# Sixteen rows of the first key load issued by ScalarE, and two w_down pieces placed ahead of the carried sum

## The chip, the core and the metric

The kernel runs on one core of one Trainium2 chip. The metric is device time in microseconds (us), the median of several executions. Beside it stands one execution that was taken with the hardware profiler. Its trace is what every duration below comes from.

## What is computed

The program is one decode step of a parallel block: `out = x + attention(xn) + glu(xn)`, with `xn` the layer norm of `x`. There are 2 batch rows of 512 values, 32 heads of 128, and attention looks at the last 2,048 positions of a key and value cache. Everything is f32. Cut to what matters:

```python
xn = layernorm(x)                                  # (2, 1, 512)
q  = (xn @ wq) split into 32 heads of 128
k, v = k_cache[:, :, 8192 - 2048:, :], v_cache[:, :, 8192 - 2048:, :]
p  = softmax(einsum("bhqd,bhkd->bhqk", q, k) * 128 ** -0.5)
a  = einsum("bhqk,bhkd->bhqd", p, v)  ->  (2, 1, 4096) @ wo
b  = ((xn @ w_gate) * (xn @ w_up)) @ w_down        # 512 -> 1376 -> 512
return x + a + b
```

Nearly all of the data is the keys and values: 2 MB for the keys of one head (both batch rows) and 2 MB for its values, each byte used once.

## The kernel before, in words

All operands except `x` in its natural layout are packed on the host into one flat `stream`, in the order in which they are loaded. `loads()` lists the loads, `placed()` says where each lands in three large SBUF tiles (`step0` to `step2`, the list `ring`), and `issue(name)` (line 486) starts one load on Sync's queue. Every load is a block of 128 rows, one for each SBUF partition.

The 32 heads are worked in 8 groups of 4. One turn of the loop at line 673 handles the keys of group `it` and the values of the group before. For a key of one head VectorE multiplies the whole tile by the query (`products`, 128 x 4096 values in place) and sums over the head dimension (`sums`). TensorE projects the queries (`project`), weighs the values (`weigh`, accumulating in PSUM tile `o_ps`), picks out the diagonal (`gather`) and multiplies by `wo` (`wo`, accumulating in PSUM tile `acc`). ScalarE computes the exponentials and copies.

Loads go in a ring: a later load overwrites the place of keys or values already used, so its issue on Sync waits for the engine that read them last. Each group of heads takes three loads of 6,144 KB. The first loads differ:

- `x` (1,057 KB): the first group of `wq`, and the small constant block with `x` transposed. Everything in the prologue (lines 516 to 539: mean, variance, `xn`, `xnb`) and the first query projection waits for it.
- `0.0` (6,080 KB): the keys of heads 0 and 1 (K0 and K1), and part of `w_gate` (`GU_A`). One of its 128 rows is 47.5 KB.
- `0.1` (5,568 KB): the keys of head 2, and the rest of `w_gate` and `w_up`.

The program is first recorded as a list of operations with their dependences, and `emit` then writes it out. `plan` works out which semaphores each operation waits for. A load with a tag (`B0`, `B1`, `B2`) counts on a semaphore shared by one place of the ring; a load without one gets a semaphore of its own. In `emit`, line 332 writes Sync's first three operations, the loads `x`, `0.0` and `0.1`, ahead of Sync's branch into its long straight block (`with nc.body("straight", ...)`, line 341). All of ScalarE's operations stand in its straight block; the first of them is the load of `x` in natural layout into `xr` (line 496, two rows of 2 KB), which waits for GpSimd's clearing of `xr`.

At the end, after the last group, Sync issues four small loads: `wo` (the last group's) and `d0` (pieces 1 to 4 of `w_down`), 1,024 KB each, `d1` (pieces 7 and 8, 512 KB) and `d2` (piece 9, 256 KB). The section `tail` (line 748) then runs in this order:

```python
    for j, i in enumerate(ROWS):                 # pieces 1 to 4, from d0
        down(i, add_rows, j, last=True)          # into acc
    dve.tensor_tensor(acc_sb, acc, xr, op=ALU.add)
    add_groups(id4, acc_sb)                      # the carried sum, into acc_g
    for i in STRIPS:                             # pieces 7, 8 (d1) and 9 (d2)
        down(i, add_groups, last=(i == STRIPS[-1]))
    dve.tensor_copy(o_out, acc_g)
```

`acc` holds four partial sums in four strips of partitions. VectorE adds `x` and moves them to SBUF (`acc_sb`), and a matrix product with `id4` adds the four strips together in `acc_g`, which lies in the PSUM tile of the queries (`q` in the profile). Each call of `add_groups` is four matrix products, one for each quarter of the output columns; the profile lists two TensorE instructions for each f32 product. The output is copied and stored by Sync.

Of the kernel before, what the change touches and what calls it, by code (L numbers as in the profile page):

```python
# [10 lines left out]
P = 128  # L11
# [18 lines left out]
EARLY, ROWS, STRIPS = (0, 5, 6, NFC), (1, 2, 3, 4), (7, 8, 9)  # L30
# [124 lines left out]
class Program:  # L155
# [131 lines left out]
    def emit(self, looped, control):  # L287
        nc, ops = self.nc, self.ops
        waits, at = self.plan(looped)
        stores = [i for i, o in enumerate(ops) if o.dma and o.args[0].space == bass.MemoryType.DRAM]  # L290
        sem = {}
        for late in (False, True):
            for i, o in enumerate(ops):
                if i in at and (i in stores) == late and o.tag not in sem:
                    sem[o.tag] = nc.alloc_semaphore(f"s_{o.tag}")
        regs = {}

        def give(i, first=None):
            o = ops[i]
            e = self.eng[o.eng]  # L300
            w = [(sem[ops[j].tag], at[j]) for j in waits[i]]
            if o.holds:
                w += [(sem[tag], regs[reg]) for tag, _, reg in o.holds]
            for s, v in w[:-1]:
                e.wait_ge(s, v)
            ins = o.call(e)
            if w:
                ins._wait_ge(*w[-1])
            if i in at:
                ins.then_inc(sem[o.tag], 16 if o.dma else 1)  # L310

        sections = {}
        for i, o in enumerate(ops):
            if o.eng == "PE":
                sec = sections.setdefault(o.place[0], {})
                if o.place in sec:
                    assert o.same(ops[sec[o.place]]), o.place
                    assert [t[::2] for t in o.holds] == [t[::2] for t in ops[sec[o.place]].holds]
                    assert (i in at) == (sec[o.place] in at)
                else:  # L320
                    sec[o.place] = i

        def run(section, *cut):
            got = list(sections[section].values())
            for i in got[cut[0] if cut else 0 : cut[1] if len(cut) > 1 else len(got)]:
                give(i)

        own = {e: [i for i, o in enumerate(ops) if o.eng == e] for e in self.eng}
        kinds = {"DVE": mybir.EngineType.DVE, "SP": mybir.EngineType.SP,
                 "ACT": mybir.EngineType.Activation}  # L330
        once = {}
        for i in own["SP"][:3]:
            give(i)
        for e in kinds:
            once[e] = self.eng[e].alloc_register(f"once_{e}")
            self.eng[e].reg_mov(once[e], 1)
            self.eng[e].br("straight")
        for i in own["POOL"]:
            give(i)
        self.eng["POOL"].br("done")  # L340
        with nc.body("straight", valid_engines=list(kinds.values())):
            for e in kinds:
                here = self.eng[e].mark_branch_hint_location()
                for i in own[e][3 if e == "SP" else 0 :]:
                    if i not in stores:
                        give(i)
                if e == "ACT":
                    far = here
                    self.eng[e].br_lt(once[e], 1, on_true="never", on_false="end")
                else:  # L350
                    if e == "SP":
                        self.eng[e].addr_align(128, offset=16, max_nops=0)
                    self.eng[e].br_lt(
                        once[e], 1, on_true="straight", on_false="end"
                    ).branch_hint(here)
        with nc.body("end", valid_engines=list(kinds.values())):
            for e in kinds:
                self.eng[e].br("done")
        control(self, regs, run)
        with nc.body("never", valid_engines=[kinds["ACT"]]):  # L360
            self.eng["ACT"].addr_align(128, offset=16, max_nops=0)
            self.eng["ACT"].br_lt(
                once["ACT"], 1, on_true="straight", on_false="done"
            ).branch_hint(far)
        nc.switch_bb("done")
        for i in stores:
            give(i)
        sp = self.eng["SP"]
        nums = sorted(s.num for t, s in sem.items() if t not in {ops[i].tag for i in stores})
        sp.sem_clear(range(nums[0], nums[-1] + 1))  # L370
        for i in stores:
            sp.wait_ge(sem[ops[i].tag], 16)
        for i in stores:
            n = sem[ops[i].tag].num
            sp.sem_clear(range(n, n + 1))
# [62 lines left out]
def build(nc, stream, x_nat, out):  # L438
    pr = Program(nc)
    pe, dve, act, pool = pr.pe, pr.dve, pr.act, pr.pool  # L440

    ring = [pr.sb(f"step{i}", [P, w]) for i, w in enumerate(TILES)]
# [36 lines left out]
    src, pos, tag_of = {}, 0, {}  # L479
    for name, (tag, _) in loads().items():  # L480
        t, lo, hi = spans[name]
# [1 line left out]
        pos += P * (hi - lo)  # L483
        tag_of[name] = tag

    def issue(name):
        t, lo, hi = spans[name]
        pr.load("SP", ring[t][:, lo:hi], src[name], tag=tag_of[name])

    issue("x")  # L490
    issue("0.0")
    issue("0.1")
    for t, v in ((mean_w, 1.0 / D), (eps_t, EPS), (ones, 1.0), (p_all, 0.0),
                 (xr, 0.0), (zero, 0.0), (mt, 0.0)):
# [18 lines left out]
    for t in (acc, *gu_ps):  # L513
        act.activation(t, ones[:, 0:1].to_broadcast([P, FB]), AF.Copy, scale=0.0,
                       tag="fold" if t is acc else "fold2")
# [22 lines left out]
        tag="qc",  # L538
# [94 lines left out]
    def add_groups(lhsT, rhs, last=False):  # L633
        nonlocal n_grp
        for j in range(4):
            pe.matmul(
                acc_g[32 * j : 32 * j + B, :], lhsT, rhs[:, j * P : (j + 1) * P],
                start=(n_grp == 0), stop=last,
            )
        n_grp += 1  # L640

    def down(c, add, *args, **kw):
        k = min(P, F - c * P)
        add(hT[:k, c % 4, c // 4, :], got["wd", c][:k], *args, **kw)
# [104 lines left out]
    for j, i in enumerate(ROWS):  # L749
        down(i, add_rows, j, last=True)  # L750
    dve.tensor_tensor(acc_sb, acc, xr, op=ALU.add)
    add_groups(id4, acc_sb)
    for i in STRIPS:
        down(i, add_groups, last=(i == STRIPS[-1]))
    dve.tensor_copy(o_out, acc_g)
    pr.load("SP", out, o_out)
    pr.emit(("q", "t", "g", "o", "w"), steer)
# [82 lines left out]
```

## Time and profile before

| | us |
|---|---|
| median of 3 runs | 376.68 |
| lowest and highest | 376.46, 378.28 |
| the profiled execution's own time | 376.57 |
| its span (first to last instruction) | 375.2 |

| engine | busy us | share of the span |
|---|---|---|
| VectorE (DVE) | 299.4 | 80% |
| TensorE matmul (PE) | 175.9 | 47% |
| TensorE weight load (PEld) | 54.8 | 15% |
| ScalarE (ACT) | 18.3 | 5% |
| GpSimd (POOL) | 3.0 | 1% |

How to read the lines below. Nearly all instructions are recorded through one helper, so nearly all carry its line, L139; they are told apart by their tiles. In a timeline line the first number is the start in us, the second the time from the first to the last of the group. `step` is the ring of loaded data, `step<-in_stream_dram` a load from the stream, `SPq` and `ACTq` the issuing queues of Sync and ScalarE. `q1` is the DMA queue that Sync's loads run on and `q10` ScalarE's; both are served by the same 16 DMA engines. A line of a windows view gives the stretch, its length, the busy time and the count of instructions of each engine, the granted TensorE clock, the mean busy share of the 16 DMA engines, and GB/s; it puts a packet where it starts, so a short stretch can show a share above 1.

### The profile page before, as it was taken

To read this page: it belongs to the slowest core of one execution; us is meant where nothing else is said; L and a number is where in the kernel's file an instruction comes from. 1 tells how busy PE (TensorE), PEld (TensorE's weight loads), DVE (VectorE), ACT (ScalarE), POOL (GpSimd) and SP (SyncE) were. 2 spreads that over 40 slices of the span, in tenths; PEclk is the share of its full clock that TensorE was granted. 3 is DMA by queue.
4 is the path that set the end of the run, shared out by engine and by line. 5 is a ranking of instruction groups with operands and counts; after the bars stand their busy time and mean duration, and the time that the engine had idled before them with its cause. 6 is when DMAs were issued, how large, how long until landed. Compare 5 with 4: busy or idle time off the path is not lost.

```text
span 375.2 us, 2080 instructions
## 1 busy us (share of the span) xinstructions
PE 175.9 (47%) x850; PEld 54.8 (15%) x850; DVE 299.4 (80%) x151; ACT 18.3 (5%) x42; POOL 3.0 (1%) x16
## 2 busy tenths in 40 slices
PE   0664743337416184064923277061740545343876
PEld 0210121002101030010400032010300112011322
DVE  0089999998599796997699985997969975999911
ACT  4000200000000000000000000000000000000000
POOL 3000000000000000000000000000000000000000
PEclk9965859587855688565695858566965869556899
DMA  9999999999999999999999999999999999999996
GB/s 365 415 456 403 447 419 419 466 456 419 419 419 419 461 461 419 419 419 419 461 461 419 419 419 419 445 472 424 419 419 419 440 477 424 419 443 394 449 401 249
DMA packets 4756, 159.62 MB, mean 425 GB/s; under 512 B 530, under 2 KB 658, under 8 KB 916
## 3 DMA queue, kind: packets, MB, share of 16 engines
q1 hardware_dynamic: 4752, 159.62, 98.8%
q10 hardware_dynamic: 4, 0.00, 0.0%
HBM read 159.55 MB, written 0.07 MB: 425 GB/s over the span
## 4 chain that ended last, share of the span: by engine, by line
DMA 49%; DVE 47%; PE 3%; issue 0%; SPq 0%; DVEq 0%
DMA step<-in_stream_dram 49%; DVE step L139 23%; DVE s L139 22%; PE q L139 2%; DVE rs L139 1%; PE acc L139 1%; SPq L139 0%; DVE acc_sb L139 0%; DVE h_sb L139 0%; PE top L139 0%; DVE nm L139 0%; DVE o_out L139 0%; DVE mt L139 0%; DVE dg L139 0%; DVE mtt L139 0%
## 5 line engine op out<-in xcount | busy, mean ns | idle before, releaser
L139 DVE TENSOR_TENSOR step<-step,q 128x4096 f32<-128x4096 f32 x32 | 141.3, 4414 | 41.7 <-DMA step<-in_stream_dram 41.7
L139 PE MATMUL o_ps<-step,p 128*32 128x512 f32 x512 | 93.0, 878 | 156.8 <-DMA step<-in_stream_dram 154.4
L139 DVE TENSOR_REDUCE s<-step 128x32 f32<-128x4096 f32 x32 | 141.3, 4417 | 0.8
L139 PEld LDWEIGHTS o_ps<-step,p 128*32 128x32 f32 x512 | 18.6, 146 | 219.0 <-DMA step<-in_stream_dram 171.7
L139 PE MATMUL q<-step,xnb 128*128 128x512 f32 x72 | 41.6, 732 | 9.0 <-DVE step L139 6.3
L139 PEld LDWEIGHTS q<-step,xnb 128*128 128x128 f32 x72 | 16.4, 240 | 28.0 <-issue 18.0
L139 PE MATMUL gu<-step,xn 128*2 128x512 f32 (+1 forms) x48 | 14.6, 774 | 11.7 <-DMA step<-in_stream_dram 11.7
L139 ACT COPY o_sb<-o_ps 128x256 f32<-128x256 f32 x16 | 5.2, 375 | 247.3 <-PE o_ps L139 247.3
L139 PE MATMUL gu<-step,o_sb 128*128 128x8 f32 x64 | 10.1, 285 | 4.0 <-ACT o_sb L139 4.0
L139 PEld LDWEIGHTS gu<-step,o_sb 128*128 128x128 f32 x64 | 9.4, 225 | 16.2 <-ACT o_sb L139 16.2
L139 ACT ACTIVATE p<-s,zero 64x128 f32<-64x128 f32 x16 | 6.4, 399 | 63.6 <-DVE s L139 63.5
L139 PE MATMUL acc<-step,oT 128*2 128x512 f32 x64 | 8.3, 592 | 0.4 <-DVE oT L139 0.4
L139 DVE TENSOR_REDUCE nm<-top 64x4 f32<-64x8 f32 x16 | 2.6, 164 | 6.8 <-PE top L139 6.7
L139 DVE RECIPROCAL rec<-tot 128x8 f32<-128x8 f32 x8 | 1.6, 198 | 6.2 <-PE tot L139 6.2
L139 PEld LDWEIGHTS gu<-step,xn 128*2 128x2 f32 x48 | 2.8, 98 | 23.3 <-DMA step<-in_stream_dram 13.4
L139 PE MATMUL top<-dg,ones 128*128 128x16 f32 x16 | 3.0, 260 | 7.0 <-DVE dg L139 7.0
L139 DVE TENSOR_REDUCE st<-xc 128x4 f32<-128x16 f32 x1 | 0.2, 169 | 6.3 <-POOL xc L139 6.3
L139 DVE TENSOR_TENSOR oT<-gu,rec 128x8 f32<-128x8 f32 x8 | 1.2, 156 | 4.3 <-PE gu L139 4.3
L139 PEld LDWEIGHTS top<-dg,ones 128*128 128x128 f32 x16 | 2.5, 188 | 12.8 <-DVE dg L139 11.8
L139 DVE TENSOR_REDUCE rs<-p 128x8 f32<-128x256 f32 x8 | 3.3, 412 | 0.9 <-ACT p L139 0.9
L139 ACT ACT_TABLE_LOAD x3 | 3.8, 1283 | 3.1 <-POOL xr L139 3.1
L139 PE MATMUL top<-st,mean_w 128*128 128x4 f32 x2 | 0.6, 364 | 6.5 <-DVE st L139 6.5
(44 smaller groups left out, 31.8 us busy)
## 6 DMA issues: line engine op xcount, KB each, us to landing
step<-in_stream_dram SPq DMA_DIRECT2D x20, 6144.0 KB, 30.5
step<-in_stream_dram SPq DMA_DIRECT2D x2, 4096.0 KB, 23.8
step<-in_stream_dram SPq DMA_DIRECT2D x1, 6080.0 KB, 19.0
step<-in_stream_dram SPq DMA_DIRECT2D x1, 5568.0 KB, 31.7
step<-in_stream_dram SPq DMA_DIRECT2D x1, 5120.0 KB, 29.8
step<-in_stream_dram SPq DMA_DIRECT2D x2, 2048.0 KB, 21.8
step<-in_stream_dram SPq DMA_DIRECT2D x2, 1024.0 KB, 11.6
step<-in_stream_dram SPq DMA_DIRECT2D x1, 1057.0 KB, 4.9
```

Of the source, the lines that this page charges most:

```text
L139: return getattr(engine, self.method)(*self.args, **self.kw)
```

## The change

There are two edits. The first: ScalarE, as its first operation and ahead of its branch, issues rows 0 to 15 of load `0.0` (on a semaphore of its own), while Sync issues `x`; Sync then issues the remaining 112 rows of `0.0` (on the shared semaphore `B0`), and `0.1`. The second: in the tail, pieces 7 and 8 of `w_down` are multiplied before the carried sum rather than after it; piece 9 stays last.

```diff
@@ -329,8 +329,10 @@
         once = {}
-        for i in own["SP"][:3]:
-            give(i)
+        first = {"ACT": 1, "SP": 3}
+        for e, n in first.items():
+            for i in own[e][:n]:
+                give(i)
         for e in kinds:
             once[e] = self.eng[e].alloc_register(f"once_{e}")
@@ -341,7 +343,7 @@
                 here = self.eng[e].mark_branch_hint_location()
-                for i in own[e][3 if e == "SP" else 0 :]:
+                for i in own[e][first.get(e, 0) :]:
                     if i not in stores:
                         give(i)
@@ -483,12 +485,14 @@
-    def issue(name):
+    def issue(name, eng="SP", rows=slice(0, P)):
         t, lo, hi = spans[name]
-        pr.load("SP", ring[t][:, lo:hi], src[name], tag=tag_of[name])
-
+        tag = tag_of[name] if rows.stop == P else None
+        pr.load(eng, ring[t][rows, lo:hi], src[name][rows], tag=tag)
+
+    issue("0.0", "ACT", slice(0, 16))
     issue("x")
-    issue("0.0")
+    issue("0.0", rows=slice(16, P))
     issue("0.1")
@@ -749,9 +753,10 @@
     dve.tensor_tensor(acc_sb, acc, xr, op=ALU.add)
+    for i in STRIPS[:-1]:
+        down(i, add_groups)
     add_groups(id4, acc_sb)
-    for i in STRIPS:
-        down(i, add_groups, last=(i == STRIPS[-1]))
+    down(STRIPS[-1], add_groups, last=True)
     dve.tensor_copy(o_out, acc_g)
```

## The prediction

> **What bounds the kernel now.** I read the page's DMA part first, then the windows, the waits behind the costliest groups, and the timeline at both ends of the span.
>
> ```profile
> span 375.2 us, 2080 instructions
> ...
> q1 hardware_dynamic: 4752, 159.62, 98.8%
> ...
> L139 DVE TENSOR_TENSOR step<-step,q 128x4096 f32<-128x4096 f32 x32 | 141.3, 4414 | 41.7 <-DMA step<-in_stream_dram 41.7
> ```
>
> Sync's queue keeps the 16 DMA engines busy for 98.8% of the span, while VectorE, the busiest compute engine, stood idle 41.7 us for loads ahead of its key products alone. In the windows:
>
> ```profile
> 0.00:1.70 1.70, 0.00 (x0) 0.00 (x0) 0.00 (x0) 0.00 (x0) 1.17 (x8) 1.00 0.00 0
> 1.70:3.10 1.40, 0.00 (x0) 0.00 (x0) 0.00 (x0) 0.04 (x1) 0.86 (x4) 1.00 0.88 199
> ...
> 371.50:375.20 3.70, 1.05 (x32) 0.74 (x32) 0.95 (x2) 0.00 (x0) 0.00 (x0) 1.00 0.07 21
> ```
>
> ```profile
> 101.23:319.20 217.97, 97.99 (x460) 30.53 (x460) 185.48 (x90) 7.22 (x20) 0.00 (x0) 0.68 1.00 433
> ```
>
> In the middle of the kernel the engines run at 433 GB/s with a share of 1.00, 433 / 16 = 27.1 GB/s each. At that rate 159.62 MB take 368.6 us. The other 6.6 us of the span lie at the ends: 1.70 us with no byte moved, a ramp of 1.40 us at 199 GB/s, 3.70 us after the stream, and small losses. So only three things can change the time: when the stream starts, whether it keeps its rate, and what follows its last byte. A load that is merely reordered changes nothing.
>
> **Part 1, the end.** The timeline of TensorE and VectorE, then that of Sync's queue for the last two loads, and the page's list of loads (KB, us from issue to landing):
>
> ```profile
> 370.36 1.04 PE L139 MATMUL acc<-step,hT 128*2 128x512 f32 x8
> 371.47 0.69 DVE L139 TENSOR_TENSOR acc_sb<-acc,xr 128x512 f32<-128x512 f32 x1 [2.31 <-PE acc L139]
> ...
> 372.21 0.40 PE L139 MATMUL q<-acc_sb,step 128*2 128x128 f32 x8 [0.81 <-DVE acc_sb L139]
> ...
> 372.43 0.84 PE L139 MATMUL q<-step,hT 128*2 128x128 f32 x24
> 373.34 0.29 DVE L139 COPY o_out<-q 128x128 f32<-128x128 f32 x1 [1.18 <-PE q L139]
> ```
>
> ```profile
> 358.11 0.91 SPq L139 DMA_DIRECT2D step<-in_stream_dram  x2
> ```
>
> ```profile
> 358.59 0.43 SPq L139 DMA_DIRECT2D step<-in_stream_dram  x1
> ```
>
> ```profile
> step<-in_stream_dram SPq DMA_DIRECT2D x1, 512.0 KB, 13.5
> step<-in_stream_dram SPq DMA_DIRECT2D x1, 256.0 KB, 13.6
> ```
>
> After the addition the carried sum takes 8 instructions and the three pieces 24. The 24 start 372.43 - 372.21 = 0.22 us after the 8, so one instruction is passed every 27.5 ns. Two of the three pieces move ahead: 16 x 27.5 ns = 0.44 us leave the chain behind the addition. They go to the time in which TensorE waits for VectorE (its 0.81 us of idle time). They need `d1`, which landed at 358.11 + 13.5 = 371.6; from there 0.44 us of issue reach 372.05, ahead of the 372.21 at which the sum can start. The cover is thus 0.16 us, and if `d1` were later by more, the sum would wait for each us beyond that. Then `d2` is next: it landed at 358.59 + 13.6 = 372.2, and the first product of piece 9 would be due at 372.21 + 0.22 = 372.43, after it by about 0.2 us. VectorE's addition reads another PSUM tile than these products write, so I add nothing for it. **End: -0.44 us**, between 0 (pieces late) and -0.44.
>
> **Part 2, the start.** The timelines of Sync's queue, ScalarE, GpSimd, TensorE and VectorE, and the loads:
>
> ```profile
> 0.74 1.32 SPq L139 DMA_DIRECT2D step<-in_stream_dram  x3
> ```
>
> ```profile
> 2.50 0.53 ACTq L139 DMA_DIRECT2D xr<-in_x_dram  x1
> ...
> 5.75 0.20 POOL L139 TENSOR_TENSOR xc<-step 128x8 f32<-128x8 f32 x1 [3.18 <-DMA step<-in_stream_dram]
> ...
> 9.79 6.08 PE L139 MATMUL q<-step,xnb 128*128 128x512 f32 x8 [2.72 <-DVE xnb L139]
> ...
> 20.29 4.42 DVE L139 TENSOR_TENSOR step<-step,q 128x4096 f32<-128x4096 f32 x1 [10.55 <-DMA step<-in_stream_dram]
> ```
>
> ```profile
> step<-in_stream_dram SPq DMA_DIRECT2D x1, 6080.0 KB, 19.0
> step<-in_stream_dram SPq DMA_DIRECT2D x1, 5568.0 KB, 31.7
> ...
> step<-in_stream_dram SPq DMA_DIRECT2D x1, 1057.0 KB, 4.9
> ```
>
> *ScalarE's issue.* It adds one issue, 0.53 us by the row of `xr`, on an engine that does nothing before 2.50, where it waits for GpSimd; it is done by about 1.3, so it costs nothing. Its branch into the straight block and the `xr` load come behind it; if that cover of 1.2 us were gone, the `xr` issue would be late, and `xr` is first read by the exponentials, which come behind the key products that begin at 20.29: nothing.
>
> *Sync's queue.* Still three issues, 1.32 us together, so `0.1` goes out no later. Its next load, `0.2`, waits for the query projection.
>
> *x gets company.* One row of `0.0` is 6080 / 128 = 47.5 KB (48,640 bytes), 48,640 / 27.1 GB/s = 1.8 us of one engine, and 16 rows over 16 engines are one row each. If the engines pass it ahead of their last rows of `x`, `x` lands up to 1.8 us later. The query would be complete at 9.79 + 6.08 + 1.8 = 17.7, still 2.6 us before K0 at 20.29, and `0.2` is issued at 17.7, while `0.1`, the third of the three issues (about 0.74 + 2/3 x 1.32 = 1.6), is on its way until about 1.6 + 31.7 = 33.3. Hidden; the cover ends at a delay of 4.4 us, and even then DMA goes on from its queue. K0 and K1 need the same bytes over the same engines, so their landing does not move: `products` and the gate products wait for two semaphores in place of one, and nothing is queued behind that wait which could run earlier.
>
> *The ramp.* ScalarE's issue can start with Sync's at 0.74. In the ramp (433 - 199) / 433 x 1.40 = 0.76 us are lost, and if the second queue filled it, that is the gain. It cannot be more, unless bytes moved before 1.70. Yet the 1.70 us before it also follow an issue that starts at 0.74, and ScalarE's cannot be earlier by much; I take **0**, with -0.76 as the one end.
>
> *The rate of the 16 rows.* The other end is a loss. No load of before has 16 rows. The nearest is `xr`, two rows of 2 KB, seen in a window of 0.4 us from 6.9 to 7.3:
>
> ```profile
> q10 hardware_dynamic: 2, 0.00, 2.6%
> ```
>
> 2.6% of 16 x 0.4 us are 0.166 us for two packets, 83 ns for 2,048 bytes or 24.6 GB/s: two engines writing neighbouring partitions went at nearly the full rate of one. But 2 KB is little, and may show only that it fits somewhere on the way. Bounds: a 128-row load gives each engine 8 rows. If nothing but the engine limits the rate, 16 rows take 1.8 us and cost nothing. If the limit of 27.1 GB/s lies at the memory, with one entry for each 8 partitions, 16 neighbouring rows have between 2 entries (16 x 1.8 / 2 = 14.4 us) and, if neighbours are dealt out in twos, 8 entries (3.6 us). Against 1.8 us that is +12.6 to +1.8 us for all engines, and since DMA is the bound it goes into the time whole. I take 0, by the row that is nearest, and keep the rest as a rival.
>
> [...]
>
> **The sum.** 376.57 (the profiled execution; 0.11 below the median of 376.68) - 0.44 + 0 + 0 = 376.13, **376.1 us**.
>
> **The rivals.** *R1, the ramp is filled.* The stream starts 0.76 us earlier and carries everything: 376.13 - 0.76 = 375.4 us. For it: 199 GB/s while both queues could have work. Against it: the second queue starts no earlier.
>
> *R2, the 16 rows share a way into memory: slower.* Its place is the first microseconds. Its price, with 4 entries, the middle of the bounds: 16 x 1.8 / 4 = 7.2 us in place of 1.8, so +5.4 us. The other 112 rows, 7 to an engine, find 12 entries that each still have 8 rows to take: 14.4 in place of 12.6 us, +1.8 us. Total 376.13 + 7.2 = 383.3 us; with 8 entries 377.9, with 2 about 388.7. It decides from a loss of 2.3 us, where it has eaten the 0.44 and the 1.9 that count as slower. For it: nothing in the rows shows that an engine, and not its target, sets 27.1 GB/s, and an edit that cuts a 128-row load leaves engines and partitions out of step. Against it: the `xr` packets. `x` would land over 5 us late and the query at about 21 or later, but K0 too would be late by the same loss. [...]
>
> *R3, it does nothing.* The pieces moved wait for `d1` past 372.21: 376.6 us, within the same band.
>
> **How the numbers follow.** A measurement of this kernel can tell about 0.5%, 1.9 us, from no change: 374.8 to 378.6. My forecast has 0.40, R1 0.12, R3 0.04, R2 in all its sizes 0.38, and 0.06 are left for what I have not seen, half of it on each side. R1 and R3 are within the band. So faster 0.03, same 0.40 + 0.12 + 0.04 = 0.56, slower 0.38 + 0.03 = 0.41. The forecast's own range is 375.4 to 376.8. The range that holds 8 in 10 must take in about two thirds of R2 (0.56 + 0.25): from 375.2 (R1 and a little) to 384.0 (R2 with 4 entries and a little).
>
> **What would show it.** Right: in the windows of the first microseconds the rate climbs as before, `xc` starts by about 7.6, the first key product stays near 20.3, the stream has 433 GB/s from 20 on and ends at 371.5; in the tail the 16 instructions of pieces 7 and 8 lie before 372.2, and the copy to `o_out` starts near 372.9 in place of 373.34. R1: a window from 1.7 to 3.1 well above 199 GB/s, and everything after about 0.8 us earlier. R2: stretches between 2 and 30 us far below 433 GB/s, K0 landing at 23 us or later, and the tail late by the same amount. Wrong in another way: TensorE waiting for `d1` or `d2` at the end, or Sync's `0.1` issued later than 2.1.

## The result, and the profile after

The changed kernel takes 393.65 us (median of 4 runs, 393.19 to 394.29) against 376.62 us for the kernel before. The ratio is 1.0447, with a 95% interval from 1.0427 to 1.0467: 17.0 us slower. The profiled execution took 393.49 us, its span is 392.2 us.

The page's first line and its DMA part (packets, MB, share of the 16 engines' span) show where to look:

```profile
span 392.2 us, 2082 instructions
...
q1 hardware_dynamic: 4736, 158.84, 97.1%
q10 hardware_dynamic: 36, 0.78, 1.6%
```

The engines are busy as before, 98.7% of a longer span, with the same bytes. So it is not that they waited for work; in some stretch they did less per microsecond. The windows of the changed kernel say which:

```profile
0.00:1.70 1.70, 0.00 (x0) 0.00 (x0) 0.00 (x0) 0.00 (x0) 1.17 (x8) 1.00 0.00 0
...
4.00:10.00 6.00, 0.00 (x0) 0.00 (x0) 0.00 (x0) 1.92 (x4) 0.00 (x0) 1.00 0.30 31
15.00:34.00 19.00, 6.57 (x10) 2.82 (x10) 0.93 (x4) 1.74 (x3) 0.61 (x4) 0.81 0.99 248
50.00:388.00 338.00, 168.43 (x786) 54.72 (x790) 285.13 (x143) 13.60 (x35) 0.00 (x0) 0.68 1.00 431
```

Read the last two columns, the share of the engines and GB/s. From 4 to 10 us few packets start, and from 3.5 to 7.2 us none at all: the 16 rows that ScalarE issued had all started by 3.5 us, and the 16 engines are still inside them (6.3 us a row, as worked out below). The share of 0.30 is low only because a packet is booked where it starts. From 15 to 34 us the engines are fully busy (0.99) at 248 GB/s in place of 433. From 50 us on the rate is the old one. The loads issued in the first 37 us, with KB and us from issue to landing:

```profile
q10 hardware_dynamic: 36, 0.78, 17.1%
issues: line engine op xcount, KB each, median us to landing
...
step<-in_stream_dram SPq DMA_DIRECT2D x1, 5320.0 KB, 36.3
...
step<-in_stream_dram SPq DMA_DIRECT2D x1, 1057.0 KB, 13.8
step<-in_stream_dram ACTq DMA_DIRECT2D x1, 760.0 KB, 11.2
```

17.1% of 16 x 37 us are 101 us for the 16 rows: 6.3 us a row, where a row of `0.0` took 1.8 us before. `x` landed after 13.8 us in place of 4.9. The timeline of ScalarE, GpSimd, TensorE and VectorE shows what that did:

```profile
0.73 0.41 ACTq L139 DMA_DIRECT2D step<-in_stream_dram  x1
...
14.59 0.20 POOL L139 TENSOR_TENSOR xc<-step 128x8 f32<-128x8 f32 x1 [12.03 <-DMA step<-in_stream_dram]
...
18.64 5.98 PE L139 MATMUL q<-step,xnb 128*128 128x512 f32 x8 [2.72 <-DVE xnb L139]
...
37.57 4.42 DVE L139 TENSOR_TENSOR step<-step,q 128x4096 f32<-128x4096 f32 x1 [18.99 <-DMA step<-in_stream_dram]
```

The query is complete at 24.6, 8.7 us later than before, but VectorE still waits another 13 us for the keys: the first product starts at 37.57 in place of 20.29, 17.3 us late, and that is the whole loss. By the trace it splits in two. `x` lands at 14.5 in place of 5.6, 8.9 us late, and since the 778 KB of the 16 rows (1.8 us at 433 GB/s) moved in that time too, the 16 rows cost 7.1 us net. From the landing of `x` to the first product it is then 37.57 - 14.54 = 23.0 us for 112 rows; before it was 20.29 - 5.64 = 14.65 us for 128, 12.8 us for 112: another 10.2 us.

The end, in contrast, came out as forecast:

```profile
388.80 0.69 DVE L139 TENSOR_TENSOR acc_sb<-acc,xr 128x512 f32<-128x512 f32 x1 [2.02 <-PE acc L139]
...
388.85 0.62 PE L139 MATMUL q<-step,hT 128*2 128x128 f32 x16
...
389.55 0.40 PE L139 MATMUL q<-acc_sb,step 128*2 128x128 f32 x8
...
389.77 0.40 PE L139 MATMUL q<-step,hT 128*2 128x128 f32 x8
390.24 0.29 DVE L139 COPY o_out<-q 128x128 f32<-128x128 f32 x1 [0.74 <-PE q L139]
```

The 16 instructions of pieces 7 and 8 run under VectorE's addition, and from the start of the addition to that of the output copy it is 1.44 us in place of 1.87. So 17.3 - 0.4 = 16.9 us of the 17.0 are accounted for.

### The profile page after: what moved, and what is told of

The parts are those of the page before. It is cut to its first block, busy times and chain, and to the rows that moved or that the text cites. A ratio compares the mean times of both kernels' runs of the same rounds, so it can differ in the third digit from the quotient of the medians.

```text
span 392.2 us, 2082 instructions
## 1 busy us (share of the span) xinstructions
PE 182.0 (46%) x850; PEld 59.5 (15%) x850; DVE 299.4 (76%) x151; ACT 18.3 (5%) x42; POOL 3.0 (1%) x16
## 4 chain that ended last, share of the span: by engine, by line
DMA 64%; PE 18%; DVE 16%; issue 1%; ACT 1%; SPq 0%; DVEq 0%
DMA step<-in_stream_dram 64%; PE q L139 8%; DVE step L139 8%; DVE s L139 7%; PE o_ps L139 6%; PE gu L139 2%; PE acc L139 2%; ACT o_sb L139 0%; PE top L139 0%; ACT p L139 0%; DVE mt L139 0%; DVE dg L139 0%; DVE acc_sb L139 0%; DVE h_sb L139 0%; DVE mtt L139 0%
## 5 line engine op out<-in xcount | busy, mean ns | idle before, releaser
L139 PE MATMUL o_ps<-step,p 128*32 128x512 f32 x512 | 92.0, 871 | 153.4 <-DMA step<-in_stream_dram 151.0
L139 PE MATMUL q<-step,xnb 128*128 128x512 f32 x72 | 48.3, 833 | 7.9 <-DVE step L139 5.1
L139 PEld LDWEIGHTS q<-step,xnb 128*128 128x128 f32 x72 | 19.0, 277 | 31.6 <-issue 21.8
L139 PE MATMUL gu<-step,xn 128*2 128x512 f32 (+1 forms) x48 | 12.8, 666 | 21.0 <-DMA step<-in_stream_dram 21.0
L139 PE MATMUL gu<-step,o_sb 128*128 128x8 f32 x64 | 11.8, 312 | 3.9 <-ACT o_sb L139 3.9
L139 PEld LDWEIGHTS gu<-step,o_sb 128*128 128x128 f32 x64 | 11.1, 261 | 16.6 <-ACT o_sb L139 16.6
## 6 DMA issues: line engine op xcount, KB each, us to landing
step<-in_stream_dram SPq DMA_DIRECT2D x1, 1057.0 KB, 13.8
```

What stands on the lines that cost most here:

```text
L139: return getattr(engine, self.method)(*self.args, **self.kw)
```

## The experiments

All start from the kernel before and have the old tail, unless the text says otherwise; the cuts of code are shortened to what matters. The ratio is to runs of the kernel before on the same chip. Four explanations compete. A: the partitions that a load writes decide its rate, because neighbouring partitions share a way into memory (SBUF). B: packets of a second queue disturb the first. C: a load that is small, or not whole, is slow in itself. D: the addresses read in HBM decide.

**The tail edit alone.** Only the last hunk of the diff.

> Theory A (the rows of a load that does not span all 128 partitions share ways into memory) and theory B (packets of a second queue throw the engines out of step) agree here: no load is changed, only two w_down pieces move ahead of the carried sum. Expected 376.62 - 0.44 = 376.2 us, ratio 0.9988; the addition of x starts 1.44 us before the output copy in place of 1.87. If the tail edit had a part in the loss, the time would lie above 376.6.

Measured: 376.11 us against 376.50, ratio 0.9995 (0.9984 to 1.0006). By the time alone it cannot be told from no change; the trace shows the 0.4 us where they were expected (addition and copy start 1.43 us apart):

```profile
371.46 0.69 DVE L139 TENSOR_TENSOR acc_sb<-acc,xr 128x512 f32<-128x512 f32 x1 [2.31 <-PE acc L139]
...
371.66 0.62 PE L139 MATMUL q<-step,hT 128*2 128x128 f32 x16 [0.26 <-DMA step<-in_stream_dram]
...
372.21 0.40 PE L139 MATMUL q<-acc_sb,step 128*2 128x128 f32 x8
...
372.89 0.29 DVE L139 COPY o_out<-q 128x128 f32<-128x128 f32 x1 [0.74 <-PE q L139]
```

TensorE waited for `d1` until 371.66, and the carried sum still starts at 372.21, as before: the cover of 0.16 us was enough. The loss is all in the first edit.

**The same cut, without the second queue.**

```diff
-    issue("0.0")
+    issue("0.0", rows=slice(0, 16))      # Sync, ahead of x
+    issue("x")
+    issue("0.0", rows=slice(16, P))      # Sync
```

> The same cut of load 0.0 into 16 and 112 rows, the 16 ahead of x, but all on Sync's queue; the tail is the old one. Theory A: the loss stays, about 394 us (376.6 + 17), with the 16 rows taking some 6 to 7 us and the 112 rows over 20. Theory B: with one queue the loss is gone, 376.6 to 377.5 us.

Measured: 392.68 us, ratio 1.0438 (1.0415 to 1.0462). The loss stays with one queue, so B is not its cause. When `x` was used, and when the first key product started:

```profile
13.13 0.20 POOL L139 TENSOR_TENSOR xc<-step 128x8 f32<-128x8 f32 x1 [10.57 <-DMA step<-in_stream_dram]
```

```profile
35.99 4.42 DVE L139 TENSOR_TENSOR step<-step,q 128x4096 f32<-128x4096 f32 x1 [18.87 <-DMA step<-in_stream_dram]
```

`x` is used 7.4 us later than before (5.75); less the 1.8 us of the bytes, the 16 rows cost 5.6 us. From there to the first product it is 22.9 us, as in the changed kernel (37.57 - 14.59 = 23.0). So of the 17.3 us by which the keys were late there, 15.7 come with the cut, and about 1.5 us more come only when the 16 rows are on a second queue beside `x`.

**The second queue, without the cut by rows.** ScalarE's share of `0.0` is cut by columns.

```diff
+    issue("0.0", "ACT", (0, 1520))       # columns, all 128 rows
     issue("x")
-    issue("0.0")
+    issue("0.0", cols=(1520, 12160))
```

> ScalarE issues beside x the same 760 KB, but as the first 1,520 columns of all 128 rows; Sync the other columns; old tail. Theory A: the loss is gone, 376.6 us (375.9 if the second queue fills the ramp), x landing within 2 us of before. Theory B: a loss of several us stays, because two queues are still served in turn: 380 us or more.

Measured: 376.87 us against 376.50, ratio 1.0011 (0.9995 to 1.0027). No loss that can be told from nothing, so the second queue did no harm here, where no load is cut by rows. And no gain: the ramp window and the first key product of this run are

```profile
1.70:3.10 1.40, 0.00 (x0) 0.00 (x0) 0.00 (x0) 0.07 (x1) 0.87 (x4) 1.00 0.93 239
```

```profile
20.32 4.42 DVE L139 TENSOR_TENSOR step<-step,q 128x4096 f32<-128x4096 f32 x1 [8.63 <-DMA step<-in_stream_dram]
```

The rate in the ramp is 239 in place of 199 GB/s, yet the keys are there at 20.32, as before (20.29).

**Halves.** Rows 0 to 63, then rows 64 to 127, both on Sync.

> Load 0.0 cut into rows 0 to 63 and rows 64 to 127, both on Sync's queue; old tail. Theory A with 16 ways of which each half reaches 8: each half takes 14.4 us in place of 7.2, together +14.4 us, less what the engines overlap: 384 to 391 us. Theory B: one queue and no small piece, 376.6 us.

Measured: 392.45 us, ratio 1.0419 (1.0399 to 1.0438): a little more than A's upper figure of 391, and 16 us above B's. The windows of this run have

```profile
10.00:34.00 24.00, 5.87 (x8) 2.23 (x8) 0.08 (x1) 0.00 (x0) 0.00 (x0) 0.74 0.94 195
```

At a share of 0.94 that is only 195 GB/s; while the engines are busy, 195 / 0.94 = 207 GB/s, 48% of 433.

**Every other row.** Two loads of 64 rows again, but the even and the odd ones:

```diff
-    issue("0.0")
+    issue("0.0", [slice(0, P, 2), slice(1, P, 2)])
```

> Load 0.0 as the 64 even rows and the 64 odd rows, both on Sync; each load reaches all 16 ways, where the halves 0 to 63 and 64 to 127 reached 8 each. Theory A in its simple form (the set of rows of a load counts): no loss, 376.6 us. Theory A in its strict form (what counts is which rows the 16 engines write at the same moment, and only a whole 128-row load is dealt out so that each engine keeps to one way): up to half the rate, up to +14.4, 377 to 391 us. Theory C: 392 us, as for the halves.

Measured: 376.46 us, ratio 1.0005 (0.9991 to 1.0020). The first product of this run starts as before:

```profile
20.28 4.42 DVE L139 TENSOR_TENSOR step<-step,q 128x4096 f32<-128x4096 f32 x1 [10.46 <-DMA step<-in_stream_dram]
```

From 7 to 19 us its windows give 401 GB/s at a share of 0.93, 431 while busy, where the halves had 207. The same number of rows, bytes and loads as the halves, and the times are 16 us apart: C falls. Nor does it take a whole 128-row load to keep the rate, as A's strict form had it.

**Eight loads of 16 rows, adjacent or stepped.**

```diff
-    issue("0.0")
+    issue("0.0", [slice(16 * n, 16 * n + 16) for n in range(8)])   # adjacent
+    issue("0.0", [slice(n, P, 8) for n in range(8)])               # stepped, in the other kernel
```

> Load 0.0 as eight loads of 16 adjacent rows, all on Sync, the same bytes and places. Theory A: each has 4 ways for 16 engines, 7.2 us in place of 1.8, eight times +5.4 = +43 us: about 420 us. Theory C: eight small loads cost the same wherever their rows lie, so the same time as the run with stepped rows.

> Load 0.0 as eight loads of 16 rows again, but each takes every eighth row (n, n+8, ... n+120); only which rows go together differs from the run with adjacent rows. Theory A: such a set has 8 ways, 3.6 us a row in place of 1.8, eight times +1.8 = +14.4 us: about 391 us, some 29 us below the adjacent ones. Theory C: the same time as the adjacent ones.

Measured: 417.16 us (ratio 1.1082, 1.1050 to 1.1114) and 393.18 us (1.0445, 1.0396 to 1.0494). The windows and the first key products, adjacent first:

```profile
10.00:54.00 44.00, 6.35 (x8) 2.42 (x8) 0.76 (x3) 0.43 (x2) 0.00 (x0) 0.62 1.08 124
```

```profile
61.30 4.42 DVE L139 TENSOR_TENSOR step<-step,q 128x4096 f32<-128x4096 f32 x1 [50.01 <-DMA step<-in_stream_dram]
```

```profile
10.00:34.00 24.00, 5.92 (x8) 2.27 (x8) 0.35 (x1) 0.00 (x0) 0.00 (x0) 0.74 0.94 195
```

```profile
36.06 4.42 DVE L139 TENSOR_TENSOR step<-step,q 128x4096 f32<-128x4096 f32 x1 [25.70 <-DMA step<-in_stream_dram]
```

The keys come 41.0 us late with adjacent rows and 15.8 us with stepped ones. Load `0.0` takes 14.4 us at full rate, so it takes 55.4 / 14.4 = 3.8 times as long and 30.2 / 14.4 = 2.1 times, as if the 16 engines had about 4 and about 8 ways. While busy, the adjacent rows had 124 / 1.08 = 115 GB/s, 27% of 433, and the stepped ones 195 / 0.94 = 207, as the halves.

**Source or destination.** In the runs so far, row p of the stream goes to partition p, so stepped partitions also mean stepped addresses in HBM. Two kernels separate them by storing the rows of this one load in another order:

```diff
-            pr.load("SP", ring[t][r, lo:hi], src[name][r], ...)
+            pr.load("SP", ring[t][r, lo:hi], src[name][slice(n, P, 8)], ...)             # r adjacent
+            pr.load("SP", ring[t][r, lo:hi], src[name][slice(16 * n, 16 * n + 16)], ...) # r stepped
```

> Eight loads of 16 rows on Sync that write 16 adjacent partitions each, but read every eighth row of the stream; the rows of this load are stored in another order, so that each value still reaches its place. If the destination (partitions of SBUF) sets the rate, as theory A says: 417 us, as in the run with adjacent rows. If the source (theory D: addresses in HBM) sets it: 393 us, as in the run with stepped rows.

> The reverse: eight loads of 16 rows that write every eighth partition, and read 16 adjacent rows of the stream. Theory A (destination): 393 us. Theory D (source): 417 us.

Measured: 417.77 us (1.1088, 1.1061 to 1.1115) and 392.71 us (1.0423, 1.0397 to 1.0448). Each time goes with the partitions written (417.16 and 393.18 before), not with the rows read: D falls.

**32 and 96 rows.** `[slice(0, 32), slice(32, P)]`, on Sync.

> Load 0.0 as rows 0 to 31 and rows 32 to 127, both on Sync. [...] Theory C (what counts is that the load is small or not whole, not where its rows lie): like the other two-piece cut, about 392 us.

Measured: 392.43 us, ratio 1.0425 (1.0373 to 1.0477). That is where C had put it, but C had already fallen with the even and odd rows.

```profile
10.00:34.00 24.00, 6.11 (x8) 2.37 (x8) 0.00 (x0) 0.00 (x0) 0.00 (x0) 0.67 0.94 204
```

The rate of this window, most of which is that of the 96 rows, is 204 GB/s (204 / 0.94 = 217 while busy), half of 433. A block of three quarters of the partitions thus went hardly faster than one of half of them (207); if A is right, it was not shown why.

**The change with other rows.** Both edits, with sets of every fourth partition in place of 16 and 112:

```diff
-    issue("0.0", "ACT", slice(0, 16))
+    issue("0.0", "ACT", (0,))            # partitions 0, 4, ... 124
     issue("x")
-    issue("0.0", rows=slice(16, P))
+    issue("0.0", turns=(1, 2, 3))        # Sync: 1, 5, ...; 2, 6, ...; 3, 7, ...
```

> Both edits of the change, with other rows: ScalarE issues partitions 0, 4, 8, ... 124 (32 rows, two for each engine) beside x, Sync the other three sets of every fourth partition, and the tail is the new one. Theory A: each set reaches all 16 ways evenly, so there is no loss; x lands up to 3.6 us late, hidden behind K0; 376.5 - 0.4 = 376.1 us, no faster than the tail edit alone, since the second queue gained nothing in the ramp with the column cut. If small sets lose by themselves: 385 us or more.

Measured: 376.06 us against 376.52, ratio 0.9986 (0.9975 to 0.9998): the loss is gone, and this is the only version whose interval lies below 1. From the tail edit alone (376.11) it cannot be told, so no gain of the first edit is shown, even with these rows. Its timeline has

```profile
7.47 0.20 POOL L139 TENSOR_TENSOR xc<-step 128x8 f32<-128x8 f32 x1 [4.90 <-DMA step<-in_stream_dram]
```

```profile
20.14 4.42 DVE L139 TENSOR_TENSOR step<-step,q 128x4096 f32<-128x4096 f32 x1 [8.68 <-DMA step<-in_stream_dram]
```

`x` is used 1.7 us later than before (5.75), within the 3.6 us expected, and the keys are there no later.

## Why the prediction was wrong

**What bounds the kernel: right.** The stream of loads is the bound and has no slack, so the 17.3 us lost at its start arrived whole at the end; the stream ran at 431 GB/s from 50 us on.

**The end: right.** -0.44 forecast, 0.43 in the trace; VectorE's addition took 0.69 us with the 16 instructions beside it, as without them.

**ScalarE's issue, Sync's queue, the ramp: right.** The issue took 0.41 us at 0.73 and held nothing up. `0.1` went out at 1.65 as before. The ramp gave almost nothing: in the cut by columns, where the second queue did no harm, its rate was 239 GB/s in place of 199, worth (239 - 199) / 433 x 1.40 = 0.13 us, and the keys were ready no sooner. That refutes R1 with its 0.76 us.

**The rate of the 16 rows: the step that failed.** I took 0, "by the row that is nearest", the two packets of `xr` at 24.6 GB/s. The measured cost is 7.1 us for the 16 rows. Two packets of 2 KB could not decide the question, and the step said so, but took their value all the same. Rows of 48,640 bytes on 16 neighbouring partitions took 6.3 us each. The forecast also had no term at all for the 112 rows that were left, and they cost 10.2 us, the larger part. This is R2 in kind: the experiments show that the destination partitions are the cause (417.77 us with neighbours written, 392.71 with every eighth, whichever rows were read), and that 16 neighbours take 3.8 times as long, as if they had 4 ways, the middle of the bounds given. It is not the cut as such that costs, as R2's reason "out of step" would have it: the even and the odd rows are such a cut too, at 376.46 us. R2 had been given 0.38, so it was no surprise as a kind of outcome, only in its size.

**R2's price: too small, and with it the range.** It had 5.4 us for the 16 rows. That is near the 5.6 us that they cost on one queue; beside `x` on a second queue it was 7.1. Above all it had 1.8 us for the other 112 rows, which was 10.2. The working there counted how many rows each way still had to take, as if all ways were in use all the time. The rates do not fit that: the 96 rows ran at 217 GB/s while busy, the 112 at about 248. No run shows the 4 and the 12 entries of that working; what the trace shows is 6.3 us a row for the 16 rows, and those 10.2 us. With 7.1 + 10.2 in place of 5.4 + 1.8 the sum gives 376.13 + 17.3 = 393.4, against 393.49 in the profiled execution from whose trace these two terms come. The upper end of 384.0 followed from the small figure. (The totals for 8 and for 2 ways, 377.9 and 388.7, leave out the 1.8 us of the 112 rows, which by the same count is due there too: 379.7 and 390.5. Neither reaches the 393.65 measured.)

**x in company: too small, but hidden as forecast.** It was 8.9 us late instead of up to 1.8, beyond the 4.4 us of cover that the prediction gave. The query was complete at 24.6, but the keys were later still, so waiting for the query cost nothing: what was lost is time of the DMA engines.

**What stays open.** Why 96 and 112 rows get little more than half the rate, and why the 16 rows cost 1.5 us more on a second queue than on one. From 7 to 19 us the even rows (401 / 0.93 = 431 GB/s while busy), the sets of every fourth row (394 / 0.91 = 433) and the whole load (422 / 0.97 = 435) all keep the full rate. The ways themselves are A's way to count: the runs show rates, but not how many ways there are or which partitions share one, and the trace does not show which engine writes which partition.

## What to carry to other kernels

In these runs a load's rate depended on which partitions it wrote: cut a large load by columns (ratio 1.0011 here), or into every second or fourth partition (1.0005 and 0.9986), but not into blocks of neighbouring partitions (16, 32 with 96, and 64 were tried: 1.1082, 1.0425 and 1.0419) nor into every eighth (1.0445), even if every byte stays the same. When the stream of loads is the bound, ask of each edit whether the 16 engines keep their rate, not only whether they have work; a busy share of 0.99 at 248 GB/s is a stall that the share does not show. And when the nearest row of a trace is far smaller than the thing to be priced, it is one end of a range and not its middle.

## What the runs showed of the hardware that was not expected

The cost of a cut follows neither the number of the pieces nor their size: two halves of 64 rows cost 16 us, the even and the odd 64 rows nothing. A piece of 96 rows was hardly faster (217 GB/s while busy) than one of 64 neighbours (207). And the slow 16 rows held up the load beside them, on their own queue and on another: `x`, itself a load of all 128 partitions, was used 7.4 us late behind the 16 rows on Sync's queue and 8.8 us late beside them on ScalarE's.
